# Slices of v issued by GpSimd, earlier places for two q tiles and a weight tile, and the copy of the means ahead of an exponential

## The chip, the cores and the metric

The kernel runs on one core of a Trainium2 chip. The metric is the device time of one execution in microseconds; the median of several runs is given. The engines are TensorE (PE in the rows, its weight loads PEld), VectorE (DVE), ScalarE (ACT), GpSimd (POOL) and SyncE (SP). Each engine works through its own list of instructions in order; SP computes nothing and only issues transfers (DMAs) between the chip's main memory and the on-chip memory.

## The reference

Three stages follow one another, all in float32; the weights come as float64.

```python
# attention: q, k, v are (2, 8, 768, 64); blocks of 32 keys, window 16
k_sum = k.reshape(B, H, nb, 32, D).max(axis=3)
v_sum = v.reshape(B, H, nb, 32, D).mean(axis=3)
scores_l = scale * q @ k.T            # kept where |i - j| < 16, else -1e9
scores_s = scale * q @ k_sum.T + log(32)
a = softmax(concat([scores_l, scores_s]))
x = a @ concat([v, v_sum])            # then (1536, 512): tokens x heads * 64
# first layer: w_in 512 x 2048, w_out 2048 x 512
h = maximum(x @ w_in, 0); x = (h * h) @ w_out
# second layer: rms norm, w_gate and w_val 512 x 1536, w_out 1536 x 512
xn = x / sqrt(mean(x * x) + 1e-6) * rms_g
out = (silu(xn @ w_gate) * (xn @ w_val)) @ w_out
```

## The kernel before

**Attention.** The 1536 tokens are 12 groups of 128, six for each of the two batches. For a group `g`, `qprep` transposes a q tile on TensorE (one tile, loaded by `qload`, serves two groups) and scales it on ScalarE; `scores` multiplies it with `kT`; `softmax` adds the mask, takes the maximum, the exponential (ScalarE) and the normalization (VectorE); `ptrans` transposes the probabilities and ScalarE copies them to `pT`; `av` multiplies them with `vx`, and the result is split into a high part (`xhi`, ScalarE) and a low part (`xlo`, VectorE). Each of the two layers multiplies with such pairs in three products.

**The tile vx.** It has four slots of 120 rows, each for 64 queries; group `g` uses slots `2g % 4` and the next, so two groups fit at a time. In a slot, 96 rows are tokens of v around the 64 queries, which `vload` brings straight from main memory in three DMAs (16, 64 and 16 tokens, all 8 heads), and 24 rows are means of blocks of v. The means of a batch come from `vmean`: twelve matmuls over three chunks `vr`, then a ScalarE copy from the accumulator to `vm`. From there `vmfix` copies them into the slots by DMA. `vload(g)` for `g > 1` can only run when `av(g-2)` has read the slots.

**Weights.** `Units` loads float64 weights in tiles of 512 KB (`load64`, `raw_wi`, `raw_wo`, ...) and converts each: two instructions on ScalarE (`x`, `u`), four on VectorE (two `tensor_scalar`, lines 182 and 183; line 186; line 189), then a copy on ScalarE and a subtraction on VectorE for the high and low part. `units1.load(n)` issues the loads of the first `n` tiles of the list.

**Order.** Within the listing below the program's order is written by hand, and the compiler's planner lays out each engine's list from it by when it expects operands to be ready; where two instructions do not depend on each other their order can change. `with after("x"):` holds the instructions in it behind the instruction marked `x`. All DMAs before the change are issued by SP, in one list. GpSimd makes the identity, the indicator matrix and the masks (`constants`) at the start and has nothing after that. The first products of layer one (`h_pair`, `y_pair`) run between the groups of attention; the rest of layer one and all of layer two follow when attention has ended.

Of the kernel before, what the change touches and what calls it, by code (L numbers as in the profile page):

```python
# [14 lines left out]
AF = mybir.ActivationFunctionType  # L15
# [17 lines left out]
def tile_window_attention_moe_moe2(  # L33
# [13 lines left out]
    nc = tc.nc  # L47
# [19 lines left out]
    NG = NT // P  # L67
# [27 lines left out]
    def constants():  # L95
        n = ind.shape[1]
        o = P // (BLK // 2) * (NC2 - 1)
        pb = BLK // 2
        nc.gpsimd.memset(ind, 1.0 / BLK)
        nc.gpsimd.affine_select(  # L100
            out=ind, in_=ind, compare_op=ALU.is_ge, fill=0.0, base=pb * o,
            pattern=[[-pb, n]], channel_multiplier=1,
        )
        nc.gpsimd.affine_select(
            out=ind, in_=ind, compare_op=ALU.is_ge, fill=0.0, base=pb - 1 - pb * o,
            pattern=[[pb, n]], channel_multiplier=-1,
        )
        nc.gpsimd.memset(um, 0.0)
        nc.gpsimd.affine_select(
            out=um, in_=um, compare_op=ALU.is_ge, fill=NEG, base=-1,  # L110
            pattern=[[1, KW + QT]], channel_multiplier=-1,
        )
        nc.gpsimd.affine_select(
            out=um, in_=um, compare_op=ALU.is_ge, fill=NEG, base=2 * WIN - 1,
            pattern=[[-1, KW + QT]], channel_multiplier=1,
        )


        mid = cpool.tile([P, NK], F32, name="mask_mid")
        nc.gpsimd.memset(mid, math.log(BLK))  # L120
        for j, n, o in ((0, WIN, 0), (K0, QT, WIN), (K1, WIN, WIN + QT)):
            nc.gpsimd.tensor_copy(mid[0:QT, j : j + n], um[0:QT, o : o + n])
            nc.gpsimd.tensor_copy(mid[QT:P, j : j + n], um[QT:P, QT + o : QT + o + n])
        first = cpool.tile([P, NK], F32, name="mask_first")
        nc.gpsimd.tensor_copy(first, mid)
        nc.gpsimd.memset(first[0:QT, 0:WIN], NEG)
        last = cpool.tile([P, NK], F32, name="mask_last")
        nc.gpsimd.tensor_copy(last, mid)
        nc.gpsimd.memset(last[QT:P, K1:NK], NEG)
        masks.update(first=first, mid=mid, last=last)  # L130
# [104 lines left out]
    def EXPACT(g):  # L235
        return g % 4 != 1

    def PARTS(g):
        return 2 if g < 3 else 1
# [15 lines left out]
    units1 = Units(order)  # L255
# [18 lines left out]
    mark = {}  # L274

    def after(*marks):
        es = ExitStack()
        for m in marks:
            es.enter_context(tc.issue_after(mark[m].ins))
        return es  # L280
# [3 lines left out]
    def psA(name, shape=None):  # L284
        tag = rot["tags"][rot["i"] % len(rot["tags"])]
        rot["i"] += 1
        pool, bufs = {"a": (psB, 2), "h": (psB, 2), "y": (psY, MT // 2), "x": (psX, 2)}[tag]
        return pool.tile(shape or [P, 512], F32, tag=tag, name=name, bufs=bufs)
# [9 lines left out]
    def token_chunk(src, b, c, nm):  # L298

        t = wpool.tile([P, 2, DM], F32, tag="w", name=nm, bufs=NW)  # L300
        for j in range(2):
            o = (2 * c + j) * P
            nc.sync.dma_start(  # L303
                t[:, j].rearrange("p (h d) -> p h d", h=H),
                src[b, :, o : o + P, :].rearrange("h p d -> p h d"),
            )
        return t
# [8 lines left out]
    def prep_k(b, c):  # L316
        ksum = state[b]
        nb1 = 2 * P // QT
        kr = state.pop(("k", b, c))
        nb2 = 2 * P // BLK  # L320
        for hf in range(2):
            ps = psA(f"kps{b}_{c}_{hf}", [P, 2, 2 * P])
            for i in range(2):
                p = 2 * hf + i
                for j in range(2):
                    nc.tensor.transpose(
                        ps[:, i, j * P : (j + 1) * P], kr[:, j, p * P : (p + 1) * P], ident
                    )
            nc.vector.tensor_reduce(
                ksum[:, 2 * hf : 2 * hf + 2, nb2 * c : nb2 * (c + 1)],  # L330
                ps.rearrange("d p (n j) -> d p n j", j=BLK),
                axis=AX.X, op=ALU.max,
            )
            nc.scalar.copy(
                kT[:, 2 * hf : 2 * hf + 2, K0 : K0 + NW1 * STEP]
                .rearrange("d p (n s) -> d p n s", s=STEP)[:, :, nb1 * c : nb1 * (c + 1), 0:QT],
                ps.rearrange("d p (n s) -> d p n s", s=QT),
            )
# [15 lines left out]
    def qload(g):  # L354
        b, r = divmod(g, GPB)
        state[("q", g)] = token_chunk(q, b, r // 2, f"qr{g}")
# [11 lines left out]
    def vmean(b, c):  # L368

        if c == 0:  # L370
            state["vmps"] = psA(f"vmean{b}", [NB, DM])
        ps = state["vmps"]
        pb = BLK // 2
        nb2 = P // pb
        vr = state.pop(("v", b, c))
        for e in range(2):
            nc.tensor.matmul(
                ps, ind[:, nb2 * (NC2 - 1 - c) : nb2 * (NC2 - 1 - c) + NB], vr[:, :, e, :],
                start=(c == 0 and e == 0), stop=(c == NC2 - 1 and e == 1),
            )  # L380
        if c == NC2 - 1:
            vm = ap_.tile([NB, DM], F32, tag="vm", name=f"vm{b}", bufs=1)
            nc.scalar.copy(vm, ps)
            state["vm"] = vm
            state[("vsum", b)] = True

# [10 lines left out]
    def vload(g):  # L397
        b, r = divmod(g, GPB)
        i0 = 2 * g % NVX
        for u in range(2):  # L400
            t0 = r * P + u * QT
            for j, n, o in ((0, WIN, t0 - WIN), (K0, QT, t0), (K1, WIN, t0 + QT)):
                o = min(max(o, 0), S - n)
                nc.sync.dma_start(  # L404
                    vx[j : j + n, i0 + u], v[b, :, o : o + n, :].rearrange("h s d -> s h d")
                )

# [18 lines left out]
    def softmax(g):  # L426
        r = g % GPB
        mk = masks["first" if r == 0 else ("last" if r == GPB - 1 else "mid")]
        sl = state.pop(("s", g))
        te = ap_.tile([P, 2, NPAIR, NK], F32, tag="t", name=f"t{g}", bufs=TB)  # L430
        t = te.rearrange("q e p n -> q (e p) n")
        state[("t", g)] = t
        mx = ap_.tile([P, H], F32, tag="mx", name=f"mx{g}", bufs=TB)
        sm = ap_.tile([P, H], F32, tag="sm", name=f"sm{g}", bufs=TB)
        parts = PARTS(g)
        n = H // parts
        for i in range(parts):
            hs = slice(n * i, n * i + n)
            tv, m_, s_ = t[:, hs], mx[:, hs], sm[:, hs]
            for e in range(2 // parts * i, 2 // parts * (i + 1)):  # L440
                nc.vector.tensor_tensor(
                    te[:, e], sl[e], mk.unsqueeze(1).to_broadcast([P, NPAIR, NK]), op=ALU.add
                )
            if EXPACT(g):
                nc.vector.reduce_max(m_, tv, axis=AX.X, negate=True)
                for h in range(hs.start, hs.stop):
                    mark[("exp", g)] = nc.scalar.activation(  # L447
                        t[:, h], t[:, h], AF.Exp, bias=mx[:, h : h + 1], accum_out=sm[:, h : h + 1]
                    )
            else:  # L450
                nc.vector.reduce_max(m_, tv, axis=AX.X)
                nc.vector.tensor_tensor(tv, tv, m_.unsqueeze(2).to_broadcast([P, n, NK]), op=ALU.subtract)
                mark[("exp", g)] = nc.scalar.activation(tv, tv, AF.Exp)
                nc.vector.reduce_sum(s_, tv, axis=AX.X)
            nc.vector.tensor_scalar_add(s_, s_, 1e-9)
            nc.vector.reciprocal(s_, s_)
            mark[("norm", g)] = nc.vector.tensor_tensor(
                tv, tv, s_.unsqueeze(2).to_broadcast([P, n, NK]), op=ALU.mult
            )
# [121 lines left out]
    def group(g):  # L581

        scores(g)
        if g > 3:
            vload(g)
        softmax(g)
        if g + 2 < NG and g % 2 == 0:
            qload(g + 2)


# [11 lines left out]
    units1.load(1)  # L602
    for c in range(NC2):
        vm_load(0, c)
    vload(0)
    vload(1)
    qload(2)
    for j in (0, LK - WIN):
        nc.gpsimd.memset(kT[:, :, j : j + WIN], 0.0)
    prep_k(0, 0)  # L610
    constants()
    prep_k(0, 1)
    prep_kend(0, 0)
    prep_k(0, 2)
# [6 lines left out]
        vmean(0, c)  # L621
    vmfix(0, NVX // 2)
    with after("vmfix"):
        units1.load(8)
    softmax(1)
    rot["tags"] = ("a", "x")
# [69 lines left out]
    for k_ in range(NK2):  # L696
        g, last = 2 * k_ + 3, 2 * k_ + 3 >= NG
# [63 lines left out]
    for i in range(n1 + 2):  # L761
        if i < n1:
# [3 lines left out]
            ps = psB.tile([P, CH], F32, tag="h", name=f"h{c}_{f}", bufs=2)  # L766
# [92 lines left out]
```

## Time and profile before

| what | value |
|---|---|
| median of 3 runs | 678.31 us (677.69 to 678.68) |
| the profiled execution, its own time | 682.7 us |
| its span, first to last instruction | 681.0 us |
| TensorE busy | 654.7 us, 96% of the span |
| VectorE busy | 404.4 us, 59% |
| ScalarE busy | 305.8 us, 45% |
| GpSimd busy | 4.1 us, 1% |
| mean granted clock of TensorE | 0.98 |

Busy time is the time in which an engine has an instruction under way. The granted clock is the share of full speed that TensorE was given. The span lies within the time of the execution, and one profiled execution need not be equal to the median.

### The profile page before, as it was taken

The numbers are of one execution on the slowest core, as the hardware profiler recorded it, in microseconds if no ns is written. First come the engines' busy times: TensorE is split into PE (matmuls) and PEld (weight loads), VectorE is DVE, ScalarE is ACT, GpSimd is POOL, SyncE is SP. The second block draws the span as 40 slices with busy tenths as digits, with TensorE's granted clock in tenths as the row PEclk, the third lists the DMA queues.
The fourth block names the chain that finished last, engine by engine and source line by source line (L and its number), as shares of the span: only waits on it lengthen the run. The fifth ranks groups of instructions, "written<-read, shape, count | busy, mean of one in ns | idle before, by whom it ended". The sixth has DMA issues, their size and how long they took to land.

```text
span 681.0 us, 9361 instructions
## 1 busy us (share of the span) xinstructions
PE 654.7 (96%) x3644; PEld 533.9 (78%) x3644; DVE 404.4 (59%) x733; ACT 305.8 (45%) x637; POOL 4.1 (1%) x25
## 2 busy tenths in 40 slices
PE   7768998999999999999999999999999999999997
PEld 5456957888888888888888888888888888888885
DVE  4799758656999579726574795189613171313132
ACT  4597558365866447326352773167411131111110
POOL 2000000000000000000000000000000000000000
PEclk9769998999999999999999999999999999999999
DMA  9678556222522223001021251015300000001011
GB/s 244 147 247 190 131 171 160 68 49 91 189 62 94 93 63 123 31 1 62 13 98 46 68 180 62 1 34 162 113 1 1 0 1 0 1 1 62 1 62 63
DMA packets 78188, 54.22 MB, mean 80 GB/s; under 512 B 46080, under 2 KB 72704, under 8 KB 78144
## 3 DMA queue, kind: packets, MB, share of 16 engines
q1 hardware_dynamic: 78144, 53.62, 26.7%
q8 instruction: 29, 0.48, 0.3%
q14 instruction: 15, 0.12, 0.1%
HBM read 50.07 MB, written 3.15 MB: 78 GB/s over the span
## 4 chain that ended last, share of the span: by engine, by line
PE 86%; SPq 5%; DVE 4%; DMA 2%; ACT 1%; issue 1%; DVEq 0%; ACTq 0%
PE y L530 19%; PE h L509 18%; PE g L509 15%; PE v L509 15%; PE z L530 14%; SPq L404 3%; PE xps L488 1%; PE pps L467 1%; PE s L418 1%; SPq L303 1%; DMA raw_wo<-in_moe_w_out_dram 1%; PE xps L500 1%; ACT t L447 1%; SPq L292 1%; DMA raw_wi<-in_moe_w_in_dram 1%
## 5 line engine op out<-in xcount | busy, mean ns | idle before, releaser
L509 PE MATMUL h<-xhi,w_wi 128*128 128x512 f32 (+1 forms) x480 | 136.6, 357 | 1.8 <-ACT xhi L478 1.2
L530 PE MATMUL y<-w_wo,hhi 128*128 128x512 f32 x384 | 120.7, 398 | 1.9 <-ACT hhi L520 1.7
L805 DVE TENSOR_TENSOR sg<-v,sg 128x512 f32<-128x512 f32 x36 | 24.9, 692 | 134.8 <-PE v L509 134.8
L509 PEld LDWEIGHTS h<-xhi,w_wi 128*128 128x128 f32 x480 | 87.3, 195 | 15.7 <-ACT xhi L478 1.9
L509 PE MATMUL v<-xhi,w_wv 128*128 128x512 f32 x288 | 95.6, 393 | 0.0
L509 PE MATMUL g<-xhi,w_wg 128*128 128x512 f32 x288 | 95.4, 393 | 0.0
L530 PE MATMUL z<-w_wp,hhiz 128*128 128x512 f32 x288 | 89.0, 392 | 0.0
L509 PE MATMUL h<-xlo,w_wi 128*128 128x512 f32 (+1 forms) x240 | 86.1, 359 | 1.8 <-DVE xlo L479 1.8
L530 PEld LDWEIGHTS y<-w_wo,hhi 128*128 128x128 f32 x384 | 72.4, 190 | 18.2 <-ACT hhi L520 1.9
L530 PE MATMUL y<-w_wo,hlo 128*128 128x512 f32 x192 | 75.1, 401 | 0.0
L803 ACT ACTIVATE sg<-g 128x512 f32<-128x512 f32 x36 | 21.6, 600 | 104.6 <-PE g L509 102.4
L509 PEld LDWEIGHTS v<-xhi,w_wv 128*128 128x128 f32 x288 | 54.0, 188 | 12.3
L509 PEld LDWEIGHTS g<-xhi,w_wg 128*128 128x128 f32 x288 | 54.0, 188 | 12.3
L530 PEld LDWEIGHTS z<-w_wp,hhiz 128*128 128x128 f32 x288 | 54.0, 188 | 11.9
L657 ACT ACTIVATE r<-h 128x512 f32<-128x512 f32 x48 | 28.7, 598 | 71.3 <-PE h L509 71.2
L509 PE MATMUL g<-xlo,w_wg 128*128 128x512 f32 x144 | 56.6, 393 | 0.0
L509 PE MATMUL v<-xlo,w_wv 128*128 128x512 f32 x144 | 56.5, 393 | 0.0
L530 PE MATMUL z<-w_wp,hloz 128*128 128x512 f32 x144 | 55.9, 392 | 0.0
L509 PEld LDWEIGHTS h<-xlo,w_wi 128*128 128x128 f32 x240 | 46.9, 195 | 9.0 <-DVE xlo L479 2.4
L658 DVE TENSOR_TENSOR r<-h,r 128x512 f32<-128x512 f32 x48 | 33.0, 687 | 35.0 <-ACT r L657 35.0
L520 ACT CAST hhiz<-sg 128x512 fp32r<-128x512 f32 x36 | 22.4, 621 | 69.7 <-DVE sg L805 69.4
L530 PEld LDWEIGHTS y<-w_wo,hlo 128*128 128x128 f32 x192 | 36.2, 191 | 8.1 <-issue 0.2
(125 smaller groups left out, 897.5 us busy)
## 6 DMA issues: line engine op xcount, KB each, us to landing
raw_wi<-in_moe_w_in_dram SPq DMA_DIRECT2D x16, 512.0 KB
raw_wo<-in_moe_w_out_dram SPq DMA_DIRECT2D x16, 512.0 KB
raw_wg<-in_moe_w_gate_dram SPq DMA_DIRECT2D x12, 512.0 KB
raw_wv<-in_moe_w_val_dram SPq DMA_DIRECT2D x12, 512.0 KB
raw_wp<-in_moe_w_out_dram SPq DMA_DIRECT2D x12, 512.0 KB
kr<-in_k_dram SPq DMA_DIRECT2D x12, 256.0 KB
qr<-in_q_dram SPq DMA_DIRECT2D x12, 256.0 KB
vr<-in_v_dram SPq DMA_DIRECT2D x6, 512.0 KB
```

Source lines behind the costliest of these rows:

```text
L292: nc.sync.dma_start(t.rearrange("p h e d -> p h (e d)"), src[b, :, 2 * P * c : 2 * P * (c + 1), :].rearrange("h (p e) d -> p h (e d)", e=2),)
L303: nc.sync.dma_start(t[:, j].rearrange("p (h d) -> p h d", h=H), src[b, :, o : o + P, :].rearrange("h p d -> p h d"),)
L404: nc.sync.dma_start(vx[j : j + n, i0 + u], v[b, :, o : o + n, :].rearrange("h s d -> s h d"))
L418: mark[("s", g)] = nc.tensor.matmul(sl[e][QT * u : QT * u + QT, p, :], qT[rr, p, QT * u : QT * u + QT], kT[rr, p, o : o + NK], start=True, ...
L447: mark[("exp", g)] = nc.scalar.activation(t[:, h], t[:, h], AF.Exp, bias=mx[:, h : h + 1], accum_out=sm[:, h : h + 1])
L509: nc.tensor.matmul(ps, a_, b_, start=(i == 0), stop=(i == tot - 1))
L520: nc.scalar.copy(hi[:, 0:n], s[:, 0:n])
L530: nc.tensor.matmul(y, a_[:, ms], b_, start=(first and i == 0), stop=(last and i == 2))
L657: nc.scalar.activation(t, ps, AF.Relu)
L658: nc.vector.tensor_tensor(t, ps, t, op=ALU.mult)
L803: nc.scalar.activation(t, psg, AF.Silu)
L805: nc.vector.tensor_tensor(t, psv, t, op=ALU.mult)
```

## The change

All DMAs of `vload` are issued by GpSimd instead of SP. The loads of groups 0 and 1, which stood between the chunks of v and q's second tile in the text, now stand behind `constants()`. The second w_in tile (`units1.load(2)`) is issued right behind q's second tile. The third q tile (`qload(4)`) is issued after `vmfix`, ahead of the list of weights, and no longer in `group(2)`. The exponentials of group 1 are held behind the copy of the means to `vm`.

```diff
-            nc.scalar.copy(vm, ps)
+            mark["vm"] = nc.scalar.copy(vm, ps)
...
-                nc.sync.dma_start(
+                nc.gpsimd.dma_start(
                     vx[j : j + n, i0 + u], v[b, :, o : o + n, :].rearrange("h s d -> s h d")
                 )
...
-                mark[("exp", g)] = nc.scalar.activation(tv, tv, AF.Exp)
+                with after(*(["vm"] if g == 1 else [])):
+                    mark[("exp", g)] = nc.scalar.activation(tv, tv, AF.Exp)
...
-        if g + 2 < NG and g % 2 == 0:
+        if g + 2 < NG and g % 2 == 0 and g > 2:
             qload(g + 2)
...
         vm_load(0, c)
-    vload(0)
-    vload(1)
     qload(2)
+    units1.load(2)
     for j in (0, LK - WIN):
         nc.gpsimd.memset(kT[:, :, j : j + WIN], 0.0)
     prep_k(0, 0)
     constants()
+    vload(0)
+    vload(1)
     prep_k(0, 1)
...
     with after("vmfix"):
+        qload(4)
         units1.load(8)
     softmax(1)
```

## Rows read from the trace of the kernel before

**Rows 1.** The page: busy tenths and TensorE's granted clock in 40 slices of 17 us.
```profile
PE   7768998999999999999999999999999999999997
...
PEclk9769998999999999999999999999999999999999
```

**Rows 2.** Stretches: us, busy us of each engine (instructions), granted clock, DMA engines' share, GB/s.
```profile
3.00:18.00 15.00, 11.95 (x116) 8.50 (x116) 7.86 (x16) 5.85 (x10) 1.74 (x10) 1.00 1.09 278
18.00:24.00 6.00, 2.64 (x7) 0.35 (x5) 4.80 (x13) 3.14 (x16) 0.00 (x0) 0.92 0.52 111
...
26.00:40.00 14.00, 11.49 (x158) 9.78 (x157) 10.29 (x25) 10.35 (x31) 0.00 (x0) 0.86 0.77 255
40.00:51.00 11.00, 7.74 (x38) 6.94 (x36) 10.57 (x22) 9.47 (x29) 0.00 (x0) 0.53 0.64 158
51.00:67.00 16.00, 13.32 (x179) 10.65 (x179) 16.00 (x29) 12.19 (x33) 0.00 (x0) 1.00 0.80 181
...
91.00:116.00 25.00, 21.11 (x212) 14.70 (x210) 20.89 (x37) 18.62 (x58) 0.00 (x0) 0.98 0.65 169
116.00:122.00 6.00, 6.00 (x52) 5.08 (x49) 4.39 (x8) 4.63 (x18) 0.00 (x0) 0.50 0.38 119
```

**Rows 3.** The chain that ended last: start us, us, what. A DMA runs from issue to landing.
```profile
22.35 3.07 DMA qr<-in_q_dram
...
48.40 2.66 DMA vx<-in_v_dram
...
94.91 4.35 DMA raw_wi<-in_moe_w_in_dram
...
107.42 6.55 DMA raw_wo<-in_moe_w_out_dram
```

**Rows 4.** TensorE in order of time: start us, us, instruction, [idle before, releaser].
```profile
19.62 1.02 PE L377 MATMUL vmean<-vr,ind 128*24 128x512 f32 x2
25.56 1.08 PE L364 MATMUL qps<-ident,qr 128*128 128x128 f32 x4 [4.91 <-DMA qr<-in_q_dram]
...
32.72 0.69 PE L488 MATMUL xps<-pT,vx 120*64 120x64 f32 x16
...
57.80 0.33 PE L488 MATMUL xps<-pT,vx 120*64 120x64 f32 x2
```

**Rows 5.** SP's issues in order of time, merged.
```profile
0.81 5.11 SPq L303 DMA_DIRECT2D kr<-in_k_dram  x6
...
13.75 8.56 SPq L404 DMA_DIRECT2D vx<-in_v_dram  x12
...
25.98 3.48 SPq L393 DMA_DIRECT2D vx<-vm  x4
...
90.73 4.08 SPq L404 DMA_DIRECT2D vx<-in_v_dram  x6
```

**Rows 6.** All issues that write vx: duration in ns, shortest, median, longest.
```profile
L404 SPq DMA_DIRECT2D vx<-in_v_dram x72: 312/606/3584, 13.8 to 142.9; - x72
```

**Rows 7.** The last instruction of GpSimd.
```profile
4.96 0.11 POOL L129 MEMSET mask_last<- 64x16 f32 x1
```

**Rows 8.** VectorE at the first addition on group 2's scores.
```profile
30.58 0.66 DVE L441 TENSOR_TENSOR t<-s,mask_mid 128x480 f32<-128x480 f32 x1 [2.49 <-PE s L418]
```

**Rows 9.** ScalarE from 24 us: group 1's exponentials and the copy of the means.
```profile
24.31 1.17 ACT L453 ACTIVATE t<-t 128x480 f32<-128x480 f32 x2 [2.58 <-DVE t L452]
25.39 0.56 ACT L383 COPY vm<-vmean 24x512 f32<-24x512 f32 x1
```

**Rows 10.** What ScalarE waited for from 84 to 120 us: us, times, longest.
```profile
ACT x_wi L175 <- DMA raw_wi<-in_moe_w_in_dram: 3.7, 2, 2.7
ACT u_wi L176 <- DVE xlo L479: 2.6, 1, 2.6
```

**Rows 11.** VectorE's conversion of weights: 38 to 67 us in ns, then 13 to 116 us.
```profile
L182 DVE TENSOR_SCALAR x_wo<-x_wo x4: 417/422/423, 47.9 to 57.3; 128x512 f32<-128x512 f32 x4
...
L186 DVE SCALAR_TENSOR_TENSOR x_wi<-raw_wi,x_wi 128x512 uint32<-128x512 uint32 x7 | 4.7, 686 | 0.0
```

## The prediction

> **What bounds the kernel now.** I read the page's slices first, then the stretches, then the chain of waits, then the queue of SyncE (SP).
>
> The slices [rows 1] show that TensorE is above 90% busy from the fifth slice on; the slices before and the one at 102 us are not full, and in most of them the granted clock is low too. The products behind cannot be shortened by a change of loads. So all that can be won lies ahead of 122 us. The stretches [rows 2] size it: from 26 to 67 us TensorE is idle 2.5 + 3.3 + 2.7 us, from 91 to 116 us 3.9 us, and from 116 to 122 us it works at a granted clock of 0.50, the lower of its two levels (1.2 of 2.4 GHz), which costs 3.0 us. Beside it stands VectorE: 10.57 of 11 us busy from 40 to 51, 16.00 of 16 from 51 to 67. In the middle of the prologue VectorE has nearly no slack, so a load that comes earlier there moves only the little that VectorE still waits.
>
> The chain of waits [rows 3] runs through SP at three places. First, the slices of v for groups 0 and 1 stand in the queue until 13.75 + 8.56 = 22.31 [rows 5]; then q's second tile is issued and lands at 25.42, and TensorE has waited 4.9 us for it [rows 4]. Second, the slices for groups 2 and 3 have been issued at 48.4 and land at 51.05. Third, at 90.73 to 94.81 [rows 5] the slices for group 7, which had to wait until av had freed their slots, hold up a w_in tile (4.35 us to landing); the vm copy stands behind that tile's conversion on ScalarE, the copies of the means behind it on SP, and a w_out tile behind them (6.55 us, to 113.97).
>
> **The change part by part.**
>
> *Loads of slices on GpSimd.* 72 issues leave SP: 24 of 64 tokens (64 x 8 heads x 64 x 4 bytes = 128 KB) and 48 of 16 (32 KB), a median 0.606 us each, between 0.312 and 3.584 [rows 6]; 72 x 0.606 = 44 us of SP's time. On GpSimd (POOL) they stand behind the constants, which end at 5.07 [rows 7], and after that POOL has no other work: a slice load that waits for av to free a slot has only later slice loads behind it. What one costs there no row shows, as POOL issues no DMA before. Below it lies the cheapest issue of SP, 0.31 us; above, the dearest, 3.58 us. I take 1.0 us, nearest to the 5.11 / 6 = 0.85 us at which SP issues half a k chunk [rows 5]: that has 128 x 8 runs of 256 bytes, more than any slice, and I put POOL somewhat above SP because nothing shows it as quick. Groups 0 and 1 are then issued from 5.1 to 17.1 us and landed, with 2.66 us as at 48.40 [rows 3], by 19.8; before it was 22.3 and later. Groups 2 and 3 can start when av(0) ends (32.72 + 0.69 = 33.4) and are landed by 33.4 + 12 + 2.7 = 48.1; av(3) starts at 57.80 today [rows 4]. Held to that, POOL keeps up as long as an issue costs under (57.8 - 33.4 - 2.66) / 12 = 1.8 us.
>
> *q's tile 2 and a w_in tile move up; q's tile 4 moves ahead of the weights.* q's tile 2 now passes the 12 slice loads, 8.56 us of SP [rows 5]. Not all of that comes back, because the 16 DMA engines were full (share 1.09) from 3 to 18 us and only about half used (0.52) from 18 to 24 [rows 2]: the slices' bytes, 2 x 4 x 32 KB + 4 x 128 KB = 0.79 MB, now compete with k, q and v's chunks. The bytes ahead of q's landing stay about the same, and the empty 0.48 x 6 = 2.9 us go: landing at 22.5 instead of 25.4, with 19.9 as the early end and 25.4 as the late one. From q's landing to the first addition on its scores VectorE took 30.58 - 25.42 = 5.2 us; 22.5 + 5.2 = 27.7, and VectorE is busy with group 1 until 30.58 - 2.49 = 28.09 [rows 8]. So its wait of 2.49 us for the scores goes whole. Against it: by 10 us POOL has moved about 5 slices, 5 x 66 KB = 0.33 MB, at 278 GB/s 1.2 us by which k, the first q tile and the first weights come later, and with them group 0's softmax, which starts the same VectorE chain. Term A: 2.49 - 1.2 = 1.3 us won (from -0.5 to 2.5). The w_in tile, 512 KB, costs 1.9 us of transfer at 278 GB/s and stands behind q's tile, so it delays nothing but the copies of the means, which have slack. q's tile 4 now passes seven weight tiles, 3.5 MB; what TensorE waits for it goes, but its first products there wait for conversions on a full VectorE, so I add nothing for it alone, and the 1.9 us by which those weights then land later are covered by the earlier start of the whole list (below).
>
> *The copy of the means first.* The copy ran at 25.39 behind both exponentials at 24.31 [rows 9]; vmean's last matmul ended at 19.62 + 1.02 = 20.64 [rows 4]. Put ahead, it can run at about 21.8, when group 0's exponentials are done. If the chunks of v come late by the full 0.79 MB at 278 GB/s, 2.8 us, vmean ends at 23.4 and the copy (0.56 us) at 24.1, still ahead of the time at which the exponentials are ready. So the added wait costs nothing up to that; behind it on ScalarE stand the exponentials, q's scaling and the copies of pT, and VectorE's sum waits for them; each us beyond is a us of the chain. The copies of the means to vx, 3.48 us of SP from 25.98 [rows 5], can then start some 2 to 3 us earlier, and the weights behind them as well.
>
> Term B, what av(0), av(2) and the weights win by this after 28 us: VectorE is idle from 26 to 40 for 3.71 us, of which 2.49 are in A, and for 0.43 from 40 to 51: 1.65 us is what can come back without moving work. I take 1.0. It is at least 0, and at most 5: TensorE's 2.7 us idle from 51 to 67 and part of what it loses at a clock of 0.53 from 40 to 51, if the planner lays conversions of weights behind 67.
>
> Term C, 91 to 122 us: SP no longer holds the w_in tile behind 4.1 us of slice loads. The tile comes up to 4 us earlier, ScalarE's waits of 3.7 us on it go [rows 10], the means and the w_out tile follow. At stake are 3.9 us idle and 3.0 us of clock. VectorE has 4.1 us free from 91 to 116, so not all can be had. I take 3.0, between 0 and 6.9.
>
> Term D, VectorE's two tensor_scalar instructions for each weight tile: at 0.42 us they take less than the 0.69 of other operations on as many elements [rows 11]. From 38 to 67 us there are 14 of them, 7 each of the two lines. If POOL's work stands in their way they wait; I take 0.5 us lost, between 0 and 14 x 0.5 = 7, half an issue each.
>
> Sum: 1.3 + 1.0 + 3.0 - 0.5 = 4.8 us. The profiled execution took 682.7 us, 1.7 more than its span of 681.0, and 4.4 more than the median of 678.31; it would come to 677.9. Against the median that is 678.3 - 4.8 = 673.5 us.
>
> **The rivals.**
>
> *R1, POOL too slow; slower.* From 1.8 us for an issue on, av(3) comes later than today. At 2.5 us, groups 0 to 3 take 24 x 2.5 = 60 us from 5.1, landing at 67.8 instead of before 57.8: 10 us lost, less 3 of term C: 678.3 + 7 = 685 us. For it: a slice is 128 or 512 runs of 256 bytes, and SP too has needed up to 3.58 us [rows 6]. Against it: SP's median of 0.61 is a third of the 1.8.
>
> *R2, VectorE held up by POOL; slower.* In 38 to 67 us 24 slice loads of 1.0 us would occupy POOL for 24 of 29 us; 14 instructions that wait 0.5 us each cost 7 us on an engine with no slack: -5.3 + 7 = 1.7, 680 us. It decides from 0.4 us each. For it: VectorE has no slack there. Against: a wait can fall on the load instead, which has slack. The Trainium skill, in SBUF — State Buffer, section Who interferes with whom, says that VectorE in a 2-port mode and GpSimd lock each other out for a whole instruction, and that moving such loads to GpSimd is the wrong way round; no row here shows it yet.
>
> *R3, hidden; no change.* The DMA engines are full to 18 us and VectorE from 40 to 67 us, so A turns to nothing, B too, and in 91 to 122 us another wait (ScalarE's 2.6 us on VectorE's xlo [rows 10]) ends at the same place: 678 us. For it: only 18 to 24 us show the DMA engines starved by SP's issues. Against: the tile at 94.91 waits for SP alone. The planner also lays the order anew, and may give back what it wins. By the Trainium skill, DMA: Bandwidth & Descriptors, section Issuing engines are not separate DMA queues, loads from several engines share the 16 DMA engines and save only the issue time; the share of 1.09 until 18 us agrees, and the 0.52 behind it shows that here issue time counts.
>
> **How the numbers follow.** 0.2%, 1.4 us, is what a measurement can tell from no change. Forecast, 1.4 to 11 us faster: 0.65. R1 0.15, R2 0.07, R3 0.13. Faster 0.65, same 0.13, slower 0.22. The likeliest case's own range: A 2.5 + B 3 + C 5.5 gives 667.3 at the low end, A 0 + B 0.4 + C 1 gives 676.9 at the high end. The range must reach into the other cases until at most 2 in 10 are left out: at the low end B at its bound of 5 gives 2.5 + 5 + 5.5 = 13, 665.5; at the high end R1 at 2.4 us an issue (5.1 + 57.6 + 2.7 = 65.4, 7.6 late, less 3) gives 683.0, which holds R2 and leaves out the dearer part of R1.
>
> **What would show it.** Right: q's tile 2 lands before 23.5 us; VectorE has no wait for scores near 28; the copy of the means lies before the exponentials of group 1; SP's wait and time on slices are gone; the w_in tile of 94.9 us is issued before 92; granted clock above 0.8 after the stretch where TensorE restarts around 116. Wrong: POOL busy with slice loads without a gap up to 60 us and TensorE waiting on vx (R1); tensor_scalar above 0.6 us (R2); the same full VectorE, ending at the same 66 us (R3). A late chunk of v that holds the copy, and so the exponentials, past 25 us would undo A.

## Result: slower by half a per cent

The kernel after takes 684.34 us (median of 20 runs, 680.93 to 689.33), the kernel before 681.62 us beside it (20 runs, 677.51 to 683.61). The ratio is 1.0054, interval 1.0035 to 1.0073: slower, where 673.5 us and 0.65 for faster had been forecast, and outside the range.

The two profiled executions must be read with care: 682.2 us after and 682.7 before, spans 680.4 and 681.0. That of after is the second quickest of its 20, that of before among the slowest of its own. Either kernel's runs spread by 6 to 8 us, and the spread goes with the mean granted clock (the kernel before beside i2: 0.987 at 676.64 us, 0.976 at 684.41). So a profile places time in a stretch, but sums are judged by the ratios alone.

The page of the kernel after: busy tenths and granted clock in 40 slices, and the queue that GpSimd's DMAs use (packets, MB, share).

```profile
PE   5879998999999999999999999999999999999997
...
POOL 6034222420000000000000000000000000000000
PEclk8859998999999999999999999999999999999999
...
q0 software_dynamic: 2688, 4.72, 2.9%
```

Against [rows 1] the losses lie at the same places: the first three slices, the third now at half clock, and the seventh, at 102 us. The stretches of the kernel after answer to [rows 2]; the last is added.

```profile
3.00:18.00 15.00, 9.02 (x66) 6.96 (x65) 4.67 (x9) 4.70 (x9) 8.85 (x24) 0.78 1.18 259
18.00:24.00 6.00, 6.00 (x28) 2.12 (x20) 4.56 (x9) 2.95 (x12) 0.00 (x0) 0.71 1.03 275
26.00:40.00 14.00, 9.32 (x106) 6.99 (x105) 13.06 (x31) 9.72 (x29) 3.46 (x6) 0.83 0.65 157
40.00:51.00 11.00, 9.29 (x75) 7.86 (x74) 10.09 (x20) 8.99 (x27) 3.85 (x6) 0.60 1.11 291
51.00:67.00 16.00, 14.78 (x195) 12.63 (x193) 15.52 (x29) 14.39 (x40) 5.90 (x11) 1.00 0.72 167
91.00:116.00 25.00, 20.89 (x209) 15.98 (x209) 18.38 (x32) 16.64 (x50) 4.17 (x8) 0.95 0.65 180
116.00:122.00 6.00, 6.00 (x54) 4.73 (x52) 4.27 (x7) 2.45 (x10) 0.06 (x1) 0.62 0.01 3
109.00:123.00 14.00, 11.21 (x87) 8.42 (x86) 8.93 (x14) 7.82 (x26) 1.06 (x2) 0.76 0.37 97
```

The DMA engines are full (share 1.18) to 18 us, and TensorE does less there, 9.02 us busy at a clock of 0.78 against 11.95 at 1.00. From 18 to 24 it does more, 6.00 us busy at 0.71 against 2.64 at 0.92. From 26 to 40 it is busy 9.32 us instead of 11.49, while VectorE's work there has grown from 10.29 to 13.06 us. The stall at 109 to 123 us is still there.

To compare kernels I use one measure, worked out from the stretches view in windows of 1 us: TensorE's loss, the length of a window less its busy time times its granted clock. It counts idle time and time at the lower clock alike. In us, with the ratio of the runs:

```
                              0-26   26-40  40-67  67-109 109-123 123-165  sum   ratio
before                         9.3    4.5    9.5    3.4    5.6     0.5    32.7   1
after                         11.0    6.3    7.1    1.7    6.1     0.0    32.2   1.0054
e1 the same lists as after     9.0    7.2    8.6    2.8    7.2     1.6    36.4   1.0057
e2 only GpSimd's issues        9.4    4.6   12.9    1.0    2.0     0.0    29.9   0.9929
f2 no early w_in tile         11.3    1.9   11.5    1.2    0.0     0.0    26.0   0.9938
j1 f2, means by GpSimd        10.7    2.6   10.6    1.2    0.0     0.0    25.0   0.9928
f4 e2, slices really held      8.9    6.0    8.9    7.9    2.0     0.1    33.8   1.0115
h1 means by GpSimd             8.8    7.5    8.2    5.6    0.0     0.0    30.1   0.9962
i1 conversion held            11.0    2.4   10.9    0.4    0.1     0.0    24.8   0.9923
i2 conversion held more       11.0    2.4    9.0    2.5    8.6     0.5    34.0   1.0089
i3 conversion held less       10.3    6.2    9.4    1.4    5.0     0.0    32.3   0.9999
p1 slices on SP, no w_in tile  7.1    6.8    7.7    1.2    7.2     1.0    31.0   1.0044
n1 both repairs                9.7    2.6    8.3    0.4    0.0     0.0    20.9   0.9878
```

How well the measure repeats shows where two versions have the same lists of instructions: e1 has those of the kernel after throughout, h1 has them up to 97 us, and up to 92 us j1 has those of f2 and n1 those of i1. There a column differs by up to 2.6 us, and the sums of e1 and the kernel after by 4.1. So the two sums of 32.7 and 32.2 can't tell before from after.

One column sorts the quick versions from the slow ones: from 109 to 123 us all with a ratio up to 0.9962 lose 2.0 us or less, all others 4.0 or more, f4 apart, whose loss lies from 67 to 109. The column 26 to 40 does not sort them by itself (h1 is quick with 7.5, i2 slow with 2.4), but it repeats within 1.2 us and is some 4 us lower in f2 and i1 than in the kernel after. The experiments are about these two.

### The profile page after: what moved, and what is told of

Same layout as the page of the kernel before. It is cut to its first block, busy times and chain, and to the rows that moved or that the text cites. A ratio compares the mean times of both kernels' runs of the same rounds, so it can differ in the third digit from the quotient of the medians.

```text
span 680.4 us, 9388 instructions
## 1 busy us (share of the span) xinstructions
PE 656.1 (96%) x3644; PEld 533.2 (78%) x3644; DVE 404.0 (59%) x733; ACT 305.6 (45%) x637; POOL 46.5 (7%) x97
## 4 chain that ended last, share of the span: by engine, by line
PE 86%; DMA 5%; DVE 4%; ACT 2%; SPq 2%; issue 1%; DVEq 0%; ACTq 0%
PE y L531 19%; PE h L510 18%; PE g L510 15%; PE v L510 15%; PE z L531 14%; DMA raw_wo<-in_moe_w_out_dram 2%; DMA raw_wi<-in_moe_w_in_dram 2%; PE xps L489 1%; PE s L418 1%; SPq L303 1%; DMA qr<-in_q_dram 1%; PE vmean L377 1%; PE xps L501 1%; PE pps L468 1%; DVE mx L445 1%; ACT t L447 1%
## 5 line engine op out<-in xcount | busy, mean ns | idle before, releaser
L510 PE MATMUL h<-xhi,w_wi 128*128 128x512 f32 (+1 forms) x480 | 133.4, 351 | 0.0
L510 PEld LDWEIGHTS h<-xhi,w_wi 128*128 128x128 f32 x480 | 84.8, 189 | 13.1 <-ACT xhi L479 0.2
L510 PE MATMUL h<-xlo,w_wi 128*128 128x512 f32 (+1 forms) x240 | 84.7, 353 | 0.0
L510 PEld LDWEIGHTS h<-xlo,w_wi 128*128 128x128 f32 x240 | 45.3, 189 | 6.5 <-issue 0.2
L404 POOL DMA_DIRECT2D vx<-in_v_dram x72 | 42.3, 595 | 93.6 <-PE xps L489 86.6
```

The costliest lines, as they stand in the source:

```text
L404: nc.gpsimd.dma_start(vx[j : j + n, i0 + u], v[b, :, o : o + n, :].rearrange("h s d -> s h d"))
L510: nc.tensor.matmul(ps, a_, b_, start=(i == 0), stop=(i == tot - 1))
```

## The experiments

Edits are against the kernel after unless another kernel is named.

### What GpSimd's issues cost, and the early sharing of the DMA engines

GpSimd's issues in the kernel after: all that write vx (ns, shortest, median, longest), then the first and two later ones in order of time.

```profile
L404 POOL DMA_DIRECT2D vx<-in_v_dram x72: 528/536/746, 2.0 to 140.5; - x72
...
2.00 2.38 POOL L404 DMA_DIRECT2D vx<-in_v_dram  x4
...
32.69 3.46 POOL L404 DMA_DIRECT2D vx<-in_v_dram  x6 [19.73 <-PE xps L489]
44.58 3.85 POOL L404 DMA_DIRECT2D vx<-in_v_dram  x6 [8.43 <-PE xps L489]
```

An issue takes 0.54 us, a little less than SP's 0.606 and far from the 1.8 at which R1 begins. But the planner put the first slices at 2.0 us, not behind the constants, so their bytes share the DMA engines with k and q from the start. First scores come at 16.8 us instead of 12.5. The first runs test whether that is the loss: e1 was to hold the slices back, e2 makes the move to GpSimd alone (an edit of the kernel before), e3 and e4 keep some or all slices on SP.

```diff
 # e1
-    vload(0)
-    vload(1)
...
     scores(0)
+    with after(("s", 0)):
+        vload(0)
+        vload(1)
 # e2, against the kernel before
-                nc.sync.dma_start(
+                nc.gpsimd.dma_start(
...
-    vload(0)
-    vload(1)
     qload(2)
...
     constants()
+    vload(0)
+    vload(1)
 # e3 (e4: nc.sync for every group), vload(0) and vload(1) behind units1.load(2)
-                nc.gpsimd.dma_start(
+                (nc.sync if g < 2 else nc.gpsimd).dma_start(
```

> The changed kernel, but the slices of groups 0 and 1 are held on GpSimd behind group 0's scores instead of going out at 2 us. T1 (early sharing: those slices took the DMA engines from k and the first q tile, so that the first scores started at 16.8 instead of 12.5 us): first scores at 12.0 to 13.0 us again, time 0.5 to 0.9% under the changed kernel, at or below the kernel before. T2 (the loss lies after 30 us, where the weights now land behind q's tile 4 and beside the slices; first w_out conversion at 44 us): start repaired but time within 0.2% of the changed kernel. T3 (the exponentials of group 1, held behind the copy of the means, 30.0 instead of 24.3 us): start repaired, exponentials at 25 to 27 us, at most 0.3% gained.

> The kernel before, with nothing changed but the slices on GpSimd (text place behind the constants). No q or weight tile moved, no held exponential. T1: all of the early loss is here, first scores near 16.8 us, time 0.4 to 0.8% above the kernel before. T2: no tile moved, so the time is at or below the kernel before. T3: as T2.

> The changed kernel, but the slices of groups 0 and 1 stay on SP, behind q's second tile and the second weight tile; all later slices on GpSimd. T1: first scores at 12.0 to 13.0 us, time 0.5 to 0.9% under the changed kernel. T2: within 0.2% of the changed kernel. T3: small gain, up to 0.3%.

> The changed kernel with all slices on SP (those of groups 0 and 1 behind q's second tile and the second weight tile): what the moved tiles and the held exponential are worth without GpSimd. T1: start as before, time 0 to 0.5% under the kernel before, above e3 by what GpSimd's queue gives later. T2 and T3: at or above the kernel before by 0.3 to 0.6%, since the moved tiles and the hold are all in it.

Measured: e1 1.0057 (1.0033 to 1.0082), e2 0.9929 (0.9906 to 0.9953), e3 0.9988 (0.9963 to 1.0014), e4 1.0044 (1.0021 to 1.0067). In e1 the slices were still issued at 2.0 us; the mark, set on an instruction of TensorE, left GpSimd's list and all others as they were, and the run is a repeat of the kernel after. e2 is the main finding of this round: GpSimd's issues by themselves gain 0.7%, early sharing and all, where T1 had expected a loss. So R1 and R2 are out, and the loss comes with the other moves. e4 shows that those moves cost 0.4% also where every slice stays on SP. e3 is 0.7% quicker than the kernel after, as T1 had it, so early sharing had to be tested once more.

A real hold needs an operand. g1 makes GpSimd read a column of q's first tile ahead of the slices; f4 does the same in e2.

```diff
     constants()
-    vload(0)
-    vload(1)
+    pace = cpool.tile([P, 1], F32, name="pace")
+    mark["pace"] = nc.gpsimd.tensor_copy(pace, state[("q", 0)][:, 1, 0:1])
+    with after("pace"):
+        vload(0)
+        vload(1)
```

> The changed kernel with a one-column GpSimd copy from q's first tile ahead of the slices of groups 0 and 1, so that they really go out only after that tile has landed (the hold in e1 did not reach the queue: they still left at 2.0 us). T1 (early sharing is what the change loses): first scores at 12.0 to 13.0 us instead of 16.8, TensorE's loss up to 18 us 4 to 5 instead of 9.3 us, time 0.4 to 0.7% under the changed kernel, as when they stayed on SP. Rival (the early loss is repaid, since TensorE loses 3 to 4 us less from 18 to 26): within 0.2% of the changed kernel.

> Only the slices on GpSimd, no tile moved, and the same real hold for groups 0 and 1. T1: the early loss of 4 us goes on top of the gain of GpSimd alone: 673 to 675 us, 1.0 to 1.3% under the kernel before. Rival (early loss repaid): 676 to 679 us. U3: a new order again, 676 to 684 us by what is lost from 109 to 123 us.

Measured: g1 1.0070 (1.0042 to 1.0097), f4 1.0115 (1.0072 to 1.0157). GpSimd in g1, in order of time:

```profile
12.61 0.19 POOL L613 COPY pace<-qr 128x1 f32<-128x1 f32 x1 [7.57 <-DMA qr<-in_q_dram]
13.20 5.65 POOL L404 DMA_DIRECT2D vx<-in_v_dram  x9 [0.41 <-issue]
21.89 1.76 POOL L404 DMA_DIRECT2D vx<-in_v_dram  x3 [3.04 <-DMA vx<-in_v_dram]
```

The hold works: in g1 TensorE's loss to 18 us falls to 4.1 us, that of the kernel before (4.2; after 9.3), in f4 to 5.5 (e2 8.2). Yet the time is no better in g1 and 1.9% worse than e2 in f4, which none of f4's expectations had. What the first scores gain is lost again by 40 us, where g1 has lost 16.8 us, the kernel after 17.4 and e1 16.2. So early sharing alone is not the cause; why e3 is quicker than g1, which has the same lists on TensorE, VectorE and ScalarE, is not shown. The price of early sharing up to 26 us is no larger than what the measure repeats to: the lists of the kernel after lose 11.0, 9.0 and 8.8 us there (after, e1, h1), the kernel before 9.3.

### One move at a time

```diff
 # f2
-    units1.load(2)
 # f3
-        if g + 2 < NG and g % 2 == 0 and g > 2:
+        if g + 2 < NG and g % 2 == 0:
...
-        qload(4)
 # k1: f2's edit and e3's
 # p1: f2's edit and e4's
```

> The changed kernel without the earlier second weight tile. So far: slices on GpSimd alone were 0.7% faster than the kernel before, while the whole change is 0.5% slower, so the moved tiles cost about 1.2% on top. U1 (the weight tile is the cause: it shares the DMA engines with v's chunks and q's second tile and holds up the copies of the means): 677 to 679 us, 0.5 to 0.7% under the kernel before. U2 (q's tile 4 ahead of the weights is the cause): 683 to 686 us, as the changed kernel. U3 (neither; any change of text gives the planner's order a new stall of TensorE between 109 and 123 us, where it lost 6.1 us in the changed kernel and 2.0 with GpSimd alone): time follows what TensorE loses in that stretch, in either direction.

> The changed kernel with q's tile 4 back in group 2, behind the weights. U1: 683 to 686 us, as the changed kernel. U2: 677 to 679 us. U3: time follows what TensorE loses from 109 to 123 us.

> The changed kernel without the earlier weight tile, and with the slices of groups 0 and 1 on SP behind q's second tile. Early sharing harmful: 673 to 676 us, since the first scores start 4 us earlier. Early sharing repaid (as the real holds, 0.2 and 1.9% slower, suggest): 677 to 682 us.

> All slices on SP and the second w_in tile at its old place: of the change only q's two tiles and the held exponential are left. If the early w_in tile is what costs in the version with all slices on SP (ratio 1.0044 there, and holding its conversion gave 1.0071), this one is at 0.996 to 1.001. If that version is slow because q's tiles pass the slices or the weights, it stays at 1.003 to 1.008 and the w_in tile is cleared for that setting.

Measured: f2 0.9938 (0.9917 to 0.9960), f3 1.0003 (0.9979 to 1.0028), k1 0.9970 (0.9947 to 0.9993), p1 1.0044 (1.0021 to 1.0066). Leaving the w_in tile at its old place takes 1.2% off the kernel after, as U1 had it; leaving q's tile 4 there, 0.5%, between U1 and U2. k1, with the first scores at 12.4 us, is 0.3% slower than f2, with 16.7, which speaks against early sharing once more. With all slices on SP the w_in tile costs nothing (e4 and p1 have the same ratio). So its price depends on the rest of the order, and one place where it acts has to be found. VectorE in the kernel after, in order of time, lines of group 1's and 2's softmax between:

```profile
27.57 0.42 DVE L182 TENSOR_SCALAR x_wi<-x_wi 128x512 f32<-128x512 f32 x1
...
29.02 0.42 DVE L183 TENSOR_SCALAR x_wi<-x_wi 128x512 uint32<-128x512 uint32 x1
...
30.49 0.69 DVE L186 SCALAR_TENSOR_TENSOR x_wi<-raw_wi,x_wi 128x512 uint32<-128x512 uint32 x1
...
31.66 0.65 DVE L441 TENSOR_TENSOR t<-s,mask_mid 128x480 f32<-128x480 f32 x1
32.22 0.68 DVE L189 CUSTOM_DVE_ANT_0 x_wi<-x_wi,u_wi 128x1024 uint16<-128x1024 uint16 x1
```

The tile that is loaded earlier is also converted earlier, and the planner lays its four VectorE instructions, 0.42 + 0.42 + 0.69 + 0.68 = 2.21 us, amid the softmax. The addition on group 2's scores has lost its wait of 2.49 us [rows 8], but it runs at 31.66 instead of 30.58. The next transposes of probabilities on TensorE show what follows. First the kernel after, then f2:

```profile
36.66 1.08 PE L468 MATMUL pps<-ident,t 128*120 128x128 f32 x4 [2.75 <-DVE sm L456]
```
```profile
34.60 0.65 PE L468 MATMUL pps<-ident,t 128*120 128x128 f32 x4
```

They come 2.06 us later, behind an idle time of 2.75 us, though the products just ahead of them start 0.8 us earlier than in f2 (33.22 against 33.98). The conversion's 2.21 us are the larger part of that idle time; the rest was not taken apart. And they take 1.08 us instead of 0.65. The stretch 34 to 40 us of the kernel after, then of i1 (below), has the clock: 0.60, a mean of which most is the lower level of 1.2 GHz (0.50), against 1.00.

```profile
34.00:40.00 6.00, 3.34 (x23) 2.73 (x24) 5.07 (x16) 5.12 (x20) 2.15 (x4) 0.60 1.06 285
```
```profile
34.00:40.00 6.00, 5.50 (x87) 4.40 (x83) 5.71 (x15) 4.60 (x15) 2.81 (x6) 1.00 1.04 278
```

### The conversion held, the tile left early

Three runs keep the early load and hold only the conversion, by marks at three places: behind group 2's exponentials (i1), group 3's (i2), and the copy of the means (i3). m1 is i1's edit in e4.

```diff
-                self.a[u] = conv_a(self.raw.pop(u), "%s%d" % u)
+                with after(*([("exp", 2)] if n[1] == 1 else [])):
+                    self.a[u] = conv_a(self.raw.pop(u), "%s%d" % u)
 # i2: ("exp", 3);  i3: "vm"
```

> The changed kernel, the second weight tile still loaded early, but its conversion on ScalarE (and so on VectorE) held behind group 2's exponentials. M1 (the tile costs time because its early landing lets the planner lay its four VectorE instructions, 2.2 us, into the softmax of groups 1 and 2): TensorE's loss from 26 to 40 us falls from 6.3 to 2 to 3 us, time 677 to 680 us, as without the earlier tile. M2 (the tile's 512 KB hold up q's second tile, v's chunks and the copy of the means on the DMA engines): 683 to 686 us, loss unchanged. M3 (only the stall of 109 to 123 us decides): time by that stretch alone, whatever 26 to 40 shows.

> The changed kernel, with the conversion of the second w_in tile held behind the exponential of group 3 instead of group 2: the tile's four VectorE instructions then come some ten instructions later still than in the run with the hold at group 2, and the list behind 45 us is laid out anew. If the conversion amid the softmax of groups 1 and 2 is the cause, any place behind that softmax will do: ratio to the kernel before 0.988 to 0.996, TensorE loses under 3.5 us from 26 to 40 (changed kernel 6.3). If the gain of the hold at group 2 was luck of the later order, this one may land anywhere up to 1.005.

> The changed kernel, with the same conversion held only behind the copy of the means: two tensor_scalar of it move behind group 1's maximum and subtraction, but all four VectorE instructions still stand ahead of group 1's sums and normalization, 2.2 us in all. If the conversion amid that softmax is the cause, this hold gives back little: ratio 1.000 to 1.006, TensorE loses 5 us or more from 26 to 40 at a granted clock below 0.9. If a hold helps whatever its place, by a new later order, the ratio is 0.990 to 0.996.

> The kernel of e4 (all tiles moved, all slices on SP; 0.44% above the kernel before), with the second weight tile's conversion held behind group 2's exponentials. M1 (the early conversion costs the time, whoever issues the slices): TensorE's loss from 26 to 40 us falls from 8.0 to under 5 us and the time to at or below the kernel before, 0 to 0.5% faster. M3 (the stall of 109 to 123 us alone decides, 6.8 us in e4): unchanged at 0.3 to 0.6% above unless that stretch falls too.

Measured: i1 0.9923 (0.9893 to 0.9952), i2 1.0089 (1.0058 to 1.0120), i3 0.9999 (0.9971 to 1.0027), m1 1.0071 (1.0047 to 1.0096). With the slices on GpSimd the local forecast held each time: i1 and i2 lose 2.4 us from 26 to 40, i3, where the conversion stays amid the softmax, 6.2. So the tile's 512 KB do no harm there, its conversion does, and it costs 4 us in that stretch. In m1, with the slices on SP, it did not hold: the loss there fell from 8.0 to 6.9 us, not under 5, and the time fell out on the wrong side too. The whole of i2 missed its expectation (0.988 to 0.996) by far. With the same 2.4 us from 26 to 40, i1 and i2 differ by 8.5 us from 109 to 123.

Nor do the 4 us reach the end. With the conversion amid the softmax TensorE has lost 24.4 to 25.9 us by 67 us (after, e1, h1, f3, i3), without it 20.5 to 24.8 (f2, j1, i1, n1, i2): most is made up from 40 to 67. The kernel after and f2 are level by then, 24.4 and 24.8; what parts them in the profiles is the late stall.

### The late stall

SP from 97 us in the kernel after, i1 and i2, in order of time:

```profile
97.27 6.15 SPq L393 DMA_DIRECT2D vx<-vm  x8
103.53 0.45 SPq L160 DMA_DIRECT2D raw_wi<-in_moe_w_in_dram  x1
104.09 0.44 SPq L164 DMA_DIRECT2D raw_wo<-in_moe_w_out_dram  x1
```
```profile
94.87 6.14 SPq L394 DMA_DIRECT2D vx<-vm  x8
101.12 0.45 SPq L164 DMA_DIRECT2D raw_wo<-in_moe_w_out_dram  x1
```
```profile
97.20 6.15 SPq L394 DMA_DIRECT2D vx<-vm  x8
103.45 1.20 SPq L164 DMA_DIRECT2D raw_wo<-in_moe_w_out_dram  x1
```

The copies of the means occupy SP for 6.15 us, and weight tiles stand behind them. What hangs on such a tile shows in the chain that ended last, of the kernel after:

```profile
104.09 6.77 DMA raw_wo<-in_moe_w_out_dram
...
110.94 0.66 ACT u_wo L176
...
112.85 0.63 ACT hhi L521
...
113.52 1.96 PE y L531 x4
```

This is the w_out wait of [rows 3], 3.3 us earlier than before and a fifth of a us longer to landing. ScalarE waits 1.7 us for the tile, and the conversion of it (`u_wo`) stands in ScalarE's list ahead of the work that leads to `hhi`; TensorE waits 2.8 us for `hhi` and then works at a clock of 0.62 (116 to 122 us, above). The first w_out issue behind the copies of the means (in h1, j1 and n1, where SP no longer issues those, the first behind 98 us) sorts the loss at 109 to 123: up to 102.0 us nothing, from 103.5 us on 2 us or more. It is the fifth w_out tile in f2, i1 and i2 and the sixth in the others; in e4, m1 and p1 the chain runs through the w_in tile issued just ahead of it.

```
issued at (us)            loss 109-123 (us)
n1 98.8                   0.0
i1 101.1  j1 101.5        0.1  0.0
f2 101.8  h1 102.0        0.0  0.0
i2 103.5  e3 103.6        8.6  8.4
after 104.1  e2 104.2     6.1  2.0
k1 105.0  i3 106.6        4.0  5.0
e1 106.6  f3 106.8        7.2  5.2
p1 107.2  before 107.4    7.2  5.6
e4 108.5  g1 109.3        6.8  7.7
m1 109.3                  6.3
f4 112.7                  2.0
```

In i2 the tile acts in another way: ScalarE waits for it, VectorE for ScalarE, and TensorE for the normalization that stands behind on VectorE.

```profile
108.94 0.66 ACT L175 ACTIVATE x_wo<-raw_wo 128x512 f32<-128x512 f32 x1 [2.14 <-DMA raw_wo<-in_moe_w_out_dram]
...
111.27 1.93 PE L469 MATMUL pps<-ident,t 128*120 128x128 f32 x8 [3.40 <-DVE t L459]
```

The table is a rule read off, and the issue time moves with all that comes before (e1 and the kernel after, with the same lists, differ by 2.5 us). h1 tests it by one edit, which sends the eight copies for batch 1 through GpSimd. j1 adds it to f2, n1 to i1.

```diff
-                mark["vmfix"] = nc.sync.dma_start(
+                mark["vmfix"] = (nc.sync if n > 1 else nc.gpsimd).dma_start(
```

> The changed kernel with the copies of batch 1's means to vx (8 issues, 6.15 us of SP from 97.3 us) on GpSimd too. P1 (two weight tiles are issued only behind them, at 103.5 and 104.1 us, and ScalarE's wait for them from 108.5 to 110.9 us is what TensorE loses from 109 to 123 us): those tiles leave SP before 100 us, loss there 6.1 -> under 3 us, time 0.4 to 0.7% under the changed kernel. P2 (those tiles have slack or the next wait ends at the same place): within 0.2% of the changed kernel.

> The changed kernel without the earlier weight tile, and with batch 1's means copied by GpSimd. P1 and P2 alike expect little, since TensorE lost nothing from 91 to 123 us without the earlier tile: 675 to 678 us. If the copies on GpSimd delay groups 6 and 7, 679 to 682 us.

> The changed kernel with both repairs: the second weight tile's conversion held, and batch 1's means copied by GpSimd. TensorE lost nothing from 91 to 123 us once the conversion was held, so if the two repairs act through one late stall they do not add: 675 to 678 us, 0.7 to 1.0% under the kernel before. If each acts by itself (1.3 and 0.9% under the changed kernel), 670 to 673 us.

Measured: h1 0.9962 (0.9939 to 0.9985), j1 0.9928 (0.9902 to 0.9953), n1 0.9878 (0.9828 to 0.9929), 674.33 us (6 runs, 668.20 to 677.31). The stretches of h1, then of n1:

```profile
91.00:109.00 18.00, 14.52 (x136) 10.19 (x138) 12.80 (x25) 13.21 (x42) 6.12 (x13) 0.91 0.78 231
109.00:123.00 14.00, 14.00 (x152) 12.04 (x145) 11.37 (x17) 9.45 (x29) 4.90 (x9) 1.00 0.18 40
```
```profile
26.00:40.00 14.00, 11.44 (x164) 8.94 (x163) 13.86 (x31) 9.95 (x29) 4.14 (x7) 1.00 0.64 157
...
91.00:109.00 18.00, 18.00 (x192) 15.32 (x191) 16.93 (x30) 15.02 (x43) 8.13 (x14) 1.00 0.79 232
109.00:123.00 14.00, 14.00 (x183) 11.71 (x184) 10.89 (x17) 8.25 (x21) 5.18 (x9) 1.00 0.28 71
```

In h1 the late stall is gone, though 3.9 us more are lost from 67 to 109 us; 0.9% of the kernel after is won, more than P1's 0.4 to 0.7. But the w_out tile did not leave SP before 100 us, as P1 had it: it is issued at 101.99, only 2.1 us earlier than in the kernel after, since behind the copies stood another wait. What SP waited for ahead of that tile in h1, VectorE's conversion of a tile before it (us, times, longest):

```profile
SPq L164 <- DVE x_wi L186: 1.6, 1, 1.6
```

j1 gains nothing over f2, whose tile was early enough already. n1 has both repairs, TensorE runs from 91 to 123 us without a gap, and it is the best version: 1.2% quicker than the kernel before by the ratio, between the two cases expected of it. Its interval still overlaps those of i1 and j1.

## Why the prediction was wrong

**The step that failed.** The prediction costed the w_in tile by its bytes alone: behind q's tile "it delays nothing but the copies of the means, which have slack". Its conversion was costed at nothing. It had VectorE's 2.49 us wait for cover, but that was the wait term A counted as won; the 2.21 us of conversion were laid into it, and TensorE lost 4 us more from 26 to 40 than in the versions without them. Left at its old place (f2), or loaded early with the conversion held (i1), the tile gives back 1.2 and 1.3%, 8 to 9 us.

These us are not the 4 us of that stretch, which are made up for the most part by 67 us. They lie in the second thing that failed, term C: the stall that was to go stayed, 6.1 us (7.2 in e1) where f2 and i1 have 0.0 and 0.1. How the earlier conversion brings the later stall is not shown: with these edits the planner lays the lists anew, and i2, where the conversion is out of the softmax, has the stall too.

**The base.** The sum started from a median of three runs, 678.31 us; twenty gave 681.62. Of the 10.8 us between forecast and result, 3.3 lie there. At the low end of the range, 678.3 - 13 is 665.3, not 665.5.

**A, +1.3.** Without that tile (f2) the loss up to 40 us is 13.2 against 13.8 before, 0.6 us won, within A's bounds but also within what the measure repeats to. With it 17.4, 16.2 and 16.3 are lost (after, e1, h1): 2.4 to 3.6 us more than before, below the bound of -0.5. Two steps of A came out otherwise. GpSimd's slices went out at 2.0 us, not at 5.1, and the first scores came 4.3 us later, where 1.2 had been reckoned; most of that was repaid by 26 us. And the sign that was to undo A appeared: the copy of the means waited for its last product until 27.3 us, later than the 25.39 before [rows 9], though group 1's exponentials then waited for VectorE and not for it.

```profile
27.31 0.58 ACT L383 COPY vm<-vmean 24x512 f32<-24x512 f32 x1 [0.48 <-PE vmean L377]
...
30.04 0.60 ACT L454 ACTIVATE t<-t 128x480 f32<-128x480 f32 x1 [0.58 <-DVE t L452]
```

**B, +1.0.** From 40 to 67 us the kernel after lost 2.4 us less than before, f2 2.1 us more, below B's bound of 0. Both are within what the measure repeats to. By 67 us A and B together, forecast at +2.3, stand at -1.2 with the tile and -1.5 without it.

**C, +3.0.** Its first steps came: slices off SP, the w_in tile issued at 89.5 us instead of 94.9, the copies of the means at 97.3 instead of 100.5, the w_out tile at 104.1 instead of 107.4. The stall did not go (6.1 against 5.6 us), and the clock from 116 to 122 us is 0.62, where above 0.8 was a sign of being right. The tile still stands behind 6.15 us of means on SP and lands 6.77 us after its issue; the prediction took the shift of the whole chain by some 3 us for 3 us won, but the stall stayed. Where the tile is issued by 102 us, C comes whole and over: f2 loses 1.2 us from 67 to 123, before 9.0.

**D, -0.5, and R2.** Next to nothing was lost. VectorE's line 182 from 13 to 116 us, in ns, and the one instruction of lines 182 and 183 that took longer, while GpSimd issues its loads from 44.58 to 48.43 us:

```profile
L182 DVE TENSOR_SCALAR x_wo<-x_wo x5: 412/416/427, 44.8 to 100.2; 128x512 f32<-128x512 f32 x5
```
```profile
45.69 0.57 DVE L183 TENSOR_SCALAR x_wi<-x_wi 128x512 uint32<-128x512 uint32 x1
```

Before, line 182 took 417 to 423 [rows 11]. The Trainium skill, in SBUF — State Buffer, section Who interferes with whom, has VectorE in a 2-port mode and GpSimd lock each other out for a whole instruction; some such delay shows here. In the 19 profiles, up to 165 us, 107 instructions of these two lines overlap a GpSimd DMA issue, and 15 of them take 455 to 681 ns, while the 430 that overlap none take 433 at most. But that is 0.26 us at most for one, and 0.15 us in all in the kernel after, where R2 needed 0.4 us for each.

**The rivals.** R1 and R2 are out by 0.54 us an issue and by e2. R3 said that C's place ends at another wait; it did, but at the weight tile behind SP's means and, with these gone (h1), at VectorE's conversions, not at VectorE's `xlo`. Without the tile the sum looks right, but by luck: f2 gains 0.62% (0.40 to 0.83), 4.2 us, where 4.8 had been forecast, but in the profiles A and B lost 1.5 us where 2.3 were to be won, and C gave 7.7 where 3.0 were.

**Open.** Why the planner's order has the late stall in the kernel after and in i2 and not in f2 and i1 is not shown. What the other moves cost with all slices on SP (p1, 0.4%) lies at q's two tiles or the held exponential and was not taken apart further; the loss from 26 to 40 is 6.8 us there without an early tile. f3 and i3 are 0.5% quicker than the kernel after with about equal sums (33.1 and 32.3 us against 32.2), a difference that the measure can't resolve. f4 is the slowest of all, with little loss from 109 to 123. No run tried the held exponential alone; leaving it out of the kernel after changes no engine's list of instructions, so it is not the cause there.

## What to carry to other kernels

A load that is moved up brings its consumers up with it: cost the conversion behind it on the engine that does it, and do not count a gap as won that the moved work can fill. When one transfer is taken out of a queue, look at what stands next ahead of the transfer that matters; here it was 6.15 us of small copies, and close behind them a wait for VectorE. Where a planner lays the lists anew after each edit, test moves singly and read the stretches to their end, since a local gain of 4 us can be gone 30 us later or sit beside a late loss of 8. And profile one program twice before columns are compared.

## What the runs showed that was not expected

GpSimd issues a slice of 128 or 512 runs in 528 to 746 ns, with little spread, where SP took 312 to 3584 [rows 6]; but twice it waited for an earlier transfer of its own (3.04 us after nine in a row in g1, 0.68 after ten in the kernel after). A load that lies late in the program's text can be issued at the very start: these came at 2.0 us, before the masks.
